# Twenty warm-up products instead of twenty-five, and a new order of work in the sixteen double steps of a gated attention mix

## The chip, the core and the metric

The kernel runs on one core of a Trainium2 chip. Its time is the device time of one execution in microseconds (us). The core has five engines that work side by side: TensorE (PE in the profile, with its weight loads as PEld), VectorE (DVE), ScalarE (ACT), GpSimd (POOL) and SyncE (SP, which here only issues DMAs). Each runs its own list of instructions in order, and they wait for each other by semaphores.

## The reference

Both branches read the same x (2048 tokens, 640 columns, 32 heads of 20):

```python
g = sigmoid((x * gate_w).sum(-1, keepdims=True))
# A: linear attention with softmax features
q, k, v = x @ wqkv                     # per head
phi(t) = concat(softmax(t @ w_phi), softmax(-t @ w_phi))
a = (phi(q) @ (phi(k).T @ v)) / (phi(q) @ sum(phi(k)) + 1e-6)   @ wo_A
# B: four segments of 512 tokens, with a memory M, z carried on
p     = softmax(q @ k.T * scale + causal mask)    # in the segment
a_mem = (phi(q) @ M) / (phi(q) @ z + 1e-6)        # phi(t) = t + 1 if t > 0 else exp(t)
o     = sigmoid(beta) * a_mem + (1 - sigmoid(beta)) * (p @ v)
M, z  = M + phi(k).T @ v, z + sum(phi(k))
b     = o @ wo_B
out   = g * a + (1 - g) * b
```

## The kernel before

The order of instructions on every engine is written out by hand; nothing is left to a scheduler.

**Start.** The weights of A's keys arrive by DMA in five blocks of rows (`wnat_k`), three from ScalarE's queue (blocks 0, 2, 4, line 98) and two from SyncE's (1, 3). While they travel, TensorE runs 25 products of zeros by zeros, 128x128 each, into two PSUM tiles in turn (`warm`, lines 316 to 318). Then a list of short names sets the order: T0 transposes block 0 (`wtp`, line 181), M0 multiplies it with the feature weights (`fold_ps`, line 189), and so on, each with a copy out of PSUM on ScalarE (a) or VectorE (d):

```python
for step in "T0a T2d M0a T1d M2a T4d M1a T3d X0 M4a M3a k0 g k1 v0 v1 r0 r1".split():
```

X0 transposes tokens (`xtp`), k and v are A's projections of keys and values (`pk`, `pv`, line 242). From k0 on TensorE runs through sixteen chunks of tokens, then A's sums (`kv_ps`), query features (`pq`) and numerators (`num`). All this is stage A, up to about 126 us.

**Stage B**, 127 to 303 us, is a loop over 16 double steps of two groups of four heads each (four double steps a segment). A double step has five bursts (`emit_burst`). A burst fills two PSUM tiles of two heads each with scores, `st_a` and then `st_b` (TensorE, line 757), and ScalarE takes exp of each (line 761, `PT`). As there are just these two tiles, the scores of the next burst wait, tile by tile, for the exps of this one. GpSimd cuts the triangles of the mask (line 768). After each burst TensorE gets filler work, and how much is written out by hand: `PLAN` has one string for each double step, a letter for each item, and `SHARES` has four numbers, the share of the double step's filler that is done after the first, second, third and fourth burst; the fifth takes the rest.

```python
whole = sum(w for w, _ in items)
for n, burst in enumerate(bursts(a, b)):
    burst()
    while items and (n == 4 or done + items[0][0] / 2 < SHARES[dstep][n] * whole):
        w, fn = items.pop(0)
        fn()
        done += w
```

The letters: `h` is half a projection of the next segment (five products of 128x320, line 943, and a copy out of PSUM on VectorE, line 949); `o` and `f` are halves of the output projections (line 887; copies and sums on VectorE, lines 896 and 898); they share two PSUM banks (`bps`). `A` and `B` are the weighted sums of v of the double step's first group and of the previous double step's last one (blocks 0 to 2, line 811), `D` and `C` their last block, the memory products (lines 819, 824) and the closing of the group (`emit_epi`: `rec`, `td` or `oB`, `mtmp` on VectorE, lines 836 to 854, all from the one PSUM tile `nda`). `k` and `q` put the exp of the key or query features on ScalarE (`ek`, line 915), `x` and `y` are the two VectorE operations that follow it (lines 918 and 919), `z` and `t` issue DMA transposes on SyncE's queue, and `u` four more at the end.

**PSUM.** In stage A a pool of four tiles of two banks is handed round (`aps`); the pools of later stages are laid over its banks in the order in which their names are listed (`num_pools`, line 594, and `b_pools`, line 712).

**After the last double step** the last group and the last four chunks of output are finished (303 to 314.8 us).

Of the kernel before, what the change touches and what calls it, by code (L numbers as in the profile page):

```python
# [15 lines left out]
def kernel(  # L16
# [84 lines left out]
    for what in "w1 w3 x0 g v0 v1".split():  # L101
        n = int(what[1:]) if len(what) > 1 else 0
# [72 lines left out]
    def w2tile(name):  # L175
        return aps.tile([P, 2, 512], F32, name=name, tag="w2")
# [137 lines left out]
        return omgh_b, CM  # L314

    warm = [w2tile("warm") for _ in range(2)]
    for n in range(25):
        nc.tensor.matmul(warm[n % 2][:, 0, 0:P], lhsT=zero_b, rhs=zero_b, start=True, stop=True)
    for step in "T0a T2d M0a T1d M2a T4d M1a T3d X0 M4a M3a k0 g k1 v0 v1 r0 r1".split():
        n = int(step[1:2] or 0)  # L320
# [259 lines left out]
    for what in "ppppvzppppdvp":  # L580
# [13 lines left out]
    nps_stack = ExitStack()  # L594
    num_pools = {n: nps_stack.enter_context(tc.tile_pool(
        name=n, bufs=2 if n == "pps" else 1, space=bass.MemoryType.PSUM, reuse_waits="tile"))
        for n in ('nps2', 'pps', 'nps0', 'nps1')}
    nps, pps = [num_pools[f"nps{n}"] for n in range(3)], num_pools["pps"]
    oTA = resB.tile([P, NCH + 1, KC, P], BF16, name="oTA")
    EARLY = 8  # L600
# [106 lines left out]
    with ExitStack() as bctx:  # L707
# [4 lines left out]
        bpt = bctx.enter_context(tc.tile_pool(name="bpt", bufs=2))  # L712
        b_pools = {n: bctx.enter_context(tc.tile_pool(
            name=n, bufs=2 if n == "bps" else 1, space=bass.MemoryType.PSUM, reuse_waits="tile"))
            for n in ('st_a', 'st_b', 'bps', 'bnd')}
        bps, st_a, bnd, st_b = [b_pools[n] for n in ("bps", "st_a", "bnd", "st_b")]
        st_pools = [st_a, st_b]

# [237 lines left out]
        def half_items(s, order):  # L956
# [11 lines left out]

        PLAN = ("qhhhhyzokxooAD", "qhhBhyChkzoxAooD", "qhhBhyChkzoxAooD",
                "ooBqoyoCokzxoADo", "hkhBhhChhqyhADztt", "khhBhxhqChfhyzAD",
                "khhBhxhqChfyzADt", "khhBhxhqChfyhzAD", "khhxtBhhqChyhADzt",
                "hhBhhqChfyhzAD", "hhBhhqCfhyzAthD", "hhBhhqhCftyhzAtD",
                "fBfCfftAD", "fBftCfftAD", "fBtfCffADf", "fBfCufAffD")
        SHARES = [[0.2, 0.42, 0.55, 0.77], [0.19, 0.4, 0.6, 0.85], [0.19, 0.4, 0.6, 0.8], [0.19, 0.4, 0.61, 0.79], [0.19, 0.38, 0.58, 0.8], [0.19, 0.41, 0.63, 0.86], [0.2, 0.4, 0.6, 0.83], [0.2, 0.4, 0.6, 0.83], [0.2, 0.4, 0.6, 0.8], [0.23, 0.39, 0.6, 0.82], [0.2, 0.39, 0.6, 0.82], [0.21, 0.39, 0.6, 0.82], [0.2, 0.4, 0.59, 0.8], [0.21, 0.39, 0.6, 0.8], [0.19, 0.37, 0.59, 0.81], [0.2, 0.41, 0.6, 0.85]]

        oT4 = oTA[:, 0:4]

# [7 lines left out]
        for dstep in range(NSEG * G // 2):  # L987
# [4 lines left out]
            items = []  # L992
            for w in PLAN[dstep]:
                if w in "hfo":
# [16 lines left out]
# [4 lines that stand above are left out]
# [156 lines left out]
```

## Time and profile before

| | us |
|---|---|
| three runs | 316.87, 316.88, 317.69; median 316.88 |
| the profiled execution | 316.55 |
| its span, first to last instruction | 314.8 |
| TensorE busy in the span | 303.3 (96%) |
| ScalarE busy | 252.2 (80%) |
| VectorE busy | 223.5 (71%) |
| GpSimd busy | 207.8 (66%) |

The granted TensorE clock of the profiled execution is 0.999. Around the span lie 316.55 - 314.8 = 1.75 us. TensorE's instructions are fetched in 33 packets of 16 KB (queue q8 of the profile). A row of the timeline gives start, length, engine, line, operation, names and count; "idle before" is how long the engine had been idle, and the name behind the arrow is what ended it.

### The profile page before, as it was taken

Reading aid. Unit: us, or ns where it says so; the run is one execution under the profiler, and the core shown is the slowest. Engines: PE = TensorE matmul, PEld = TensorE weight load, DVE = VectorE, ACT = ScalarE, POOL = GpSimd, SP = SyncE. Lnnn points to the kernel's source line nnn. Section 1 sums busy time; section 2 is a strip of 40 time slices with the busy share of each in tenths; the row PEclk is TensorE's granted clock in tenths of the full one; section 3 lists DMA queues with packets and bytes.
Section 4 is the critical chain, followed back from the end, with each engine's and each line's share of the span. In section 5 each row is a group of like instructions: output and inputs, shape, how many; then the busy total and the mean of one; then the engine's idle time right before and its main releaser. Section 6 shows DMA issues by size and latency. Waiting matters only on the chain.

```text
span 314.8 us, 10102 instructions
## 1 busy us (share of the span) xinstructions
PE 303.3 (96%) x4183; PEld 208.0 (66%) x4187; DVE 223.5 (71%) x508; ACT 252.2 (80%) x320; POOL 207.8 (66%) x308
## 2 busy tenths in 40 slices
PE   8999999999999999999999999999999999999994
PEld 7788877755578788465566566665666666566573
DVE  3487997998779997568767677876765765354562
ACT  4677888267856548999998999999899898998852
POOL 7588599004248989857647476888786867666550
PEclk9999999999999999999999999999999999999999
DMA  7979934439118889774421394474744544231132
GB/s 227 196 176 201 217 100 135 123 106 364 53 35 120 132 127 154 139 96 81 59 46 35 69 127 85 79 100 83 96 91 70 89 91 77 65 83 48 53 81 85
DMA packets 94008, 34.58 MB, mean 110 GB/s; under 512 B 82442, under 2 KB 93834, under 8 KB 93962
## 3 DMA queue, kind: packets, MB, share of 16 engines
q1 hardware_dynamic: 93386, 33.28, 53.6%
q8 instruction: 33, 0.54, 0.7%
q10 hardware_dynamic: 576, 0.66, 0.7%
q14 instruction: 13, 0.11, 0.1%
HBM read 6.10 MB, written 2.62 MB: 28 GB/s over the span
## 4 chain that ended last, share of the span: by engine, by line
PE 67%; ACT 22%; DVE 6%; POOL 2%; issue 2%; ACTq 0%; DVEq 0%; POOLq 0%
ACT PT L761 19%; PE st_ps L757 9%; PE proj L887 9%; PE proj L943 9%; PE pk L242 7%; PE pq L420 7%; PE pv L242 7%; PE nda L811 6%; PE proj L557 3%; DVE tt L527 2%; PE num L478 2%; DVE rr L503 2%; PE kv_ps L393 2%; POOL oA L686 1%; PE nda L819 1%
## 5 line engine op out<-in xcount | busy, mean ns | idle before, releaser
L761 ACT ACTIVATE PT<-st_ps 128x1024 bf16<-128x1024 f32 x160 | 153.7, 1023 | 12.6 <-PE st_ps L757 10.2
L768 POOL TENSOR_SCALAR_AFFINE_SELECT PT<-PT 128x512 bf16<-128x512 bf16 (+1 forms) x130 | 87.0, 688 | 45.6 <-ACT PT L761 45.4
L811 PEld LDWEIGHTS <-PT 128*128 128x128 bf16 x1280 | 40.0, 96 | 9.5 <-issue 5.6
L811 PE MATMUL nda<-vB,PT 128*128 128x21 bf16 x1240 | 41.6, 173 | 0.1
L261 POOL TENSOR_TENSOR EkSn<-Ek,krec 128x1280 bf16<-128x1280 bf16 x15 | 35.1, 2357 | 9.0 <-DVE krec L260 7.1
L949 DVE CAST Z<-proj 128x320 bf16<-128x320 f32 x44 | 21.0, 488 | 23.4 <-PE proj L943 22.5
L943 PEld LDWEIGHTS <-xTf 128*128 128x128 bf16 x300 | 26.4, 97 | 14.2 <-issue 5.7
L427 ACT ACTIVATE Eq<-pq 128x1024 bf16<-128x1024 f32 x20 | 19.4, 1021 | 12.3 <-PE pq L420 12.3
L257 DVE TENSOR_REDUCE ksum<-Ek 128x64 f32<-128x1280 bf16 x16 | 23.6, 1474 | 7.2 <-ACT Ek L253 7.2
L887 PE MATMUL proj<-WkA,oTA 128*128 128x320 bf16 x160 | 28.2, 300 | 0.0
L527 DVE TENSOR_TENSOR tt<-num,rr 128x640 f32<-128x640 f32 x32 | 24.9, 812 | 4.4 <-POOL rr L520 1.7
L686 POOL TENSOR_TENSOR oA<-tt 128x640 bf16<-128x640 f32 x16 | 24.6, 1541 | 5.2 <-DVE tt L527 5.0
L757 PE MATMUL st_ps<-Z 32*128 32x512 bf16 (+3 forms) x256 | 24.7, 299 | 3.2 <-ACT PT L761 2.2
L253 ACT ACTIVATE Ek<-pk 128x640 bf16<-128x640 f32 x32 | 20.8, 703 | 7.9 <-PE pk L242 6.8
L757 PE MATMUL st_ps<-Eq 32*128 32x512 bf16 (+3 forms) x256 | 25.1, 299 | 1.9 <-ACT PT L761 1.4
L242 PEld LDWEIGHTS <-xTf 128*128 128x128 bf16 x200 | 22.7, 113 | 4.7
L420 PE MATMUL pq<-xTf,WqA 128*128 128x512 bf16 x96 | 22.0, 379 | 0.4 <-issue 0.3
L851 POOL TENSOR_TENSOR oB<-td 128x320 bf16<-128x320 f32 x22 | 18.9, 861 | 5.0 <-DVE td L848 5.0
L887 PE MATMUL proj<-WvA,oT 128*128 128x320 bf16 x120 | 21.0, 300 | 0.0
L848 DVE TENSOR_TENSOR td<-nda,rec 128x640 f32<-128x640 f32 x23 | 19.0, 825 | 2.5 <-DVE rec L838 0.5
L557 PEld LDWEIGHTS <-xTf 128*128 128x128 bf16 x180 | 15.8, 97 | 4.6
L887 PEld LDWEIGHTS <-oTA 128*128 128x128 bf16 x160 | 13.6, 97 | 8.0 <-issue 4.0
(183 smaller groups left out, 553.5 us busy)
## 6 DMA issues: line engine op xcount, KB each, us to landing
Z<-EkSn SPq DMA_DIRECT2D x32, 160.0 KB, 2.7
out_dram<-orow SPq DMA_DIRECT2D x8, 160.0 KB, 1.8
out_dram<-oTA SPq DMA_DIRECT2D x6, 160.0 KB, 1.9
WvA<-in_A_wqkv_dram SPq DMA_DIRECT2D x2, 400.0 KB, 6.2
WvB<-in_B_wv_dram SPq DMA_DIRECT2D x1, 800.0 KB, 4.7
WkB<-in_B_wk_dram SPq DMA_DIRECT2D x1, 800.0 KB, 6.5
WqB<-in_B_wq_dram SPq DMA_DIRECT2D x1, 800.0 KB, 8.3
WkA<-in_A_wo_dram SPq DMA_DIRECT2D x1, 800.0 KB, 11.3
```

The source lines that it names most:

```text
L242: nc.tensor.matmul(ps[:, bk, 0:n], lhsT=key_tokens(c, sc), rhs=rhs, start=(c == 0), stop=(c == by_row[-1][0] if sc == 0 and W is WkA else ...
L261: (nc.vector if sc == NCH - 1 else nc.gpsimd).tensor_tensor(out=EkSn[:, sc].rearrange("p s (h f) -> p (s h) f", f=DH), in0=Ek.rearrange("p ...
L420: nc.tensor.matmul(pq[:, half, :], lhsT=WqA[:, c, j * P:(j + 1) * P], rhs=xq[:, 2 * qb + half, c], start=(c == 0), stop=(c == KC - 1))
L527: nc.vector.tensor_tensor(out=tt[:, sgn].rearrange("p (b h) d -> p b h d", b=2), in0=ps, in1=csb, op=ALU.mult)
L557: nc.tensor.matmul(ps, lhsT=xq[:, sc // 4, cc, sc % 4 * P:(sc % 4 + 1) * P], rhs=W[:, cc, half * 320:(half + 1) * 320], start=(cc == 0), s ...
L686: nc.gpsimd.tensor_tensor(out=oA.rearrange("p (h d) -> p h d", d=DH), in0=tt[:, 0], in1=tt[:, 1], op=ALU.add)
L757: nc.tensor.matmul(ps[:, i - i0, o:o + L - c * P], lhsT=kT[32 * i:32 * i + 32, c * P:(c + 1) * P], rhs=qT[32 * i:32 * i + 32, c * P:L], st ...
L761: nc.scalar.activation(out=PT[:, i0:i0 + 2], in_=ps, func=ACT.Exp, scale=SCALE_B)
L768: nc.gpsimd.affine_select(out=v, in_=v, pattern=[[0, n_i], [1, P]], compare_op=ALU.is_ge, fill=0.0, base=0, channel_multiplier=-1)
L811: nc.tensor.matmul(nd[:, j, i], lhsT=block(st, c)[:, i, (j - c) * P:(j - c + 1) * P], rhs=vB[:, c, 4 * st.g + i, :], start=(c == 0), stop= ...
L887: nc.tensor.matmul(ps, lhsT=oT[:, k % KC], rhs=W[:, k % KC, hs], start=(k == 0), stop=(k == n - 1))
L943: nc.tensor.matmul(ps, lhsT=xq[:, sc // 4, k, sc % 4 * P:(sc % 4 + 1) * P], rhs=W[:, k, half * 320:(half + 1) * 320], start=(k == 0), stop ...
```

## The change

- The loop of warm-up products runs 20 times, not 25. TensorE's list gets ten instructions shorter (a load and a product each), so that each border between packets of instructions falls ten instructions later in the work.
- The last warm-up product now goes to the other of the two `warm` tiles. Through the rest of stage A, banks 0 and 1 change places with banks 6 and 7 in every tile. In the lists of pools two names are exchanged (`nps1` with `nps2`, `bnd` with `st_a`), which gives the later pools the same exchange: every PSUM tile of after follows the same tile as before.
- `PLAN` is written anew in double steps 0 to 7, 11 to 13 and 15, and `SHARES` in all but 6 and 8. The letters are the same in sum. One `h` moves from double step 6 to 4, one `t` from 11 to 12. Seven times a letter with work for VectorE moves ahead of an item that ends with a copy out of PSUM: `y` ahead of an `h` in 0, 1 and 2, `x` ahead of an `o` in 2 and of an `h` in 5, 6 and 7. ScalarE's order of instructions stays as it is.

```diff
-    for n in range(25):
+    for n in range(20):
...
-        for n in ('nps2', 'pps', 'nps0', 'nps1')}
+        for n in ('nps1', 'pps', 'nps0', 'nps2')}
...
-            for n in ('st_a', 'st_b', 'bps', 'bnd')}
+            for n in ('bnd', 'st_b', 'bps', 'st_a')}
...
-        PLAN = ("qhhhhyzokxooAD", "qhhBhyChkzoxAooD", "qhhBhyChkzoxAooD",
-                "ooBqoyoCokzxoADo", "hkhBhhChhqyhADztt", "khhBhxhqChfhyzAD",
-                "khhBhxhqChfyzADt", "khhBhxhqChfyhzAD", "khhxtBhhqChyhADzt",
-                "hhBhhqChfyhzAD", "hhBhhqCfhyzAthD", "hhBhhqhCftyhzAtD",
-                "fBfCfftAD", "fBftCfftAD", "fBtfCffADf", "fBfCufAffD")
-        SHARES = [[0.2, 0.42, 0.55, 0.77], [0.19, 0.4, 0.6, 0.85], [0.19, 0.4, 0.6, 0.8], [0.19, 0.4, 0.61, 0.79], [0.19, 0.38, 0.58, 0.8], [0.19, 0.41, 0.63, 0.86], [0.2, 0.4, 0.6, 0.83], [0.2, 0.4, 0.6, 0.83], [0.2, 0.4, 0.6, 0.8], [0.23, 0.39, 0.6, 0.82], [0.2, 0.39, 0.6, 0.82], [0.21, 0.39, 0.6, 0.82], [0.2, 0.4, 0.59, 0.8], [0.21, 0.39, 0.6, 0.8], [0.19, 0.37, 0.59, 0.81], [0.2, 0.41, 0.6, 0.85]]
+        PLAN = ("qhhhyzhokxooAD", "qhhByhChkzoxAooD", "qhhByhChkzxoAooD",
+                "ooBqoyokCozxoADo", "hkhBhhChhqhyAhDztt", "khhBxhhqChfhyzAD",
+                "khhBxhhqCfyzADt", "khhBxhhqChfyhzAD", "khhxtBhhqChyhADzt",
+                "hhBhhqChfyhzAD", "hhBhhqCfhyzAthD", "hhBhhqhCftyhzAD",
+                "fBftCfftAD", "ffBtCfftAD", "fBtfCffADf", "fBCuffAffD")
+        SHARES = [[0.2, 0.42, 0.55, 0.78], [0.19, 0.4, 0.6, 0.84], [0.2, 0.4, 0.6, 0.81], [0.19, 0.38, 0.59, 0.78], [0.19, 0.38, 0.58, 0.81], [0.18, 0.41, 0.65, 0.86], [0.2, 0.4, 0.6, 0.83], [0.19, 0.4, 0.6, 0.83], [0.2, 0.4, 0.6, 0.8], [0.22, 0.39, 0.6, 0.82], [0.19, 0.39, 0.61, 0.82], [0.2, 0.39, 0.6, 0.82], [0.2, 0.4, 0.6, 0.8], [0.21, 0.4, 0.61, 0.8], [0.19, 0.37, 0.59, 0.82], [0.2, 0.41, 0.6, 0.84]]
```

## The prediction

> **What bounds the kernel.** The chain that ended last (section 4 of the page) comes first:
>
> ```profile
> PE 67%; ACT 22%; DVE 6%; POOL 2%; issue 2%; ACTq 0%; DVEq 0%; POOLq 0%
> ```
>
> It lies on TensorE for two thirds of the span, so I looked at the two places that the change touches. The first is the start, in the timeline of TensorE, 0 to 7.6 us:
>
> ```profile
> 1.06 2.85 PE L318 MATMUL warm<-zero_b 128*128 128x128 bf16 x25 [1.06 <-DVE zero_b L125]
> 3.70 1.27 PE L181 MATMUL wtp<-ident_b,wnat_k 128*128 128x128 bf16 x10
> 5.22 0.82 PE L189 MATMUL fold_ps<-Wphi,WkT 128*128 128x140 bf16 x10 [0.25 <-ACT WkT L183]
> 5.84 0.74 PE L181 MATMUL wtp<-ident_b,wnat_k 128*128 128x128 bf16 x5
> 6.37 0.76 PE L189 MATMUL fold_ps<-Wphi,WkT 128*128 128x140 bf16 x10
> 6.97 0.44 PE L181 MATMUL wtp<-ident_b,wnat_k 128*128 128x128 bf16 x5
> ```
>
> The transposes T0 and T2 follow the warm-up products without a hole, M0 waits for T0's copy, and five transposes take 0.74 us at 5.84 and 0.44 us at 6.97: between them TensorE got faster.
>
> The second place is stage B. The busy times of each engine in the stretches between the first exps of the double steps (columns: PE, PEld, DVE, ACT, POOL, clock, DMA share, GB/s; here double steps 3, 4, 6, 8, 10 and 12):
>
> ```profile
> 159.03:169.81 10.78, 10.42 (x155) 6.42 (x154) 8.33 (x22) 10.20 (x12) 6.44 (x12) 1.00 0.15 31
> 169.81:180.78 10.97, 10.74 (x159) 6.71 (x159) 6.24 (x16) 10.16 (x12) 6.67 (x14) 1.00 0.27 49
> ...
> 192.15:203.29 11.14, 10.67 (x165) 6.92 (x164) 8.31 (x18) 10.82 (x14) 8.91 (x14) 1.00 0.45 87
> ...
> 214.73:225.71 10.98, 10.23 (x161) 6.50 (x161) 8.12 (x18) 10.52 (x14) 9.10 (x15) 1.00 0.64 89
> ...
> 237.00:248.47 11.47, 11.37 (x170) 7.38 (x168) 7.71 (x17) 10.31 (x12) 8.42 (x15) 1.00 0.43 72
> ...
> 259.92:271.31 11.39, 11.37 (x167) 7.20 (x166) 5.35 (x12) 9.70 (x11) 8.47 (x17) 1.00 0.35 73
> ```
>
> TensorE and ScalarE are both nearly full. In 10 and 12 TensorE never rests and ScalarE does for 1.2 to 1.7 us; in 6 and 8, where ScalarE has two feature exps, it rests for 0.3 to 0.5 us. Neither engine alone sets the length. The timeline of ScalarE in double step 10 shows how:
>
> ```profile
> 237.00 1.94 ACT L761 ACTIVATE PT<-st_ps 128x1024 bf16<-128x1024 f32 x2 [0.20 <-PE st_ps L757]
> 239.53 3.87 ACT L761 ACTIVATE PT<-st_ps 128x1024 bf16<-128x1024 f32 x4 [0.59 <-PE st_ps L757]
> 243.29 0.74 ACT L915 ACTIVATE ek<-Z 128x640 bf16<-128x640 bf16 x1
> 244.09 1.94 ACT L761 ACTIVATE PT<-st_ps 128x1024 bf16<-128x1024 f32 x2
> 246.28 1.94 ACT L761 ACTIVATE PT<-st_ps 128x1024 bf16<-128x1024 f32 x2 [0.26 <-POOL Mbd L858]
> ```
>
> Two exps take 1.94 us, then ScalarE waits for scores when the filler before them was too long (0.59 us after the first burst). On TensorE the opposite: in the burst at 236.51 the four scores of the second tile wait 0.23 us for the exps before. Two rules follow. Where ScalarE was idle, filler that is d longer makes the next exps d later. Where a second tile waits for exps, filler restarts from their end, so lateness up to that wait is swallowed.
>
> **The start.** Five products go, 0.107 us apart (25 from 1.06 to 3.70): 0.53 us. Not all is on the path. The landing record of the first weight block is at 3.38, so T0 moves from 3.70 to about 3.41. The second block lands at 4.15, so T2 can begin at 4.20 rather than 4.23. M0 waits for the copy of T0, which goes from 4.48 to 4.19, so M0 starts at 4.93 rather than 5.22: 0.29 us. From the starts of single products a column costs 0.84 ns up to 6.87 us and 0.43 ns after. If that turn stays where it is, TensorE arrives there 0.27 us ahead in slow work, which is 0.14 us of fast work. I take 0.2 us, bounds 0.14 and 0.29. TensorE then works with no pause to 52 us (busy 42.86 of 42.86 us from 9.24 on), and the later inputs landed well ahead (tokens 6.79 for use at 7.91, values' weights 10.53 for 12.39 and later), so nothing swallows it.
>
> The Trainium skill (TensorE: Matmul & The Clock Gate, Why this matters for your kernels) asks for at least 4 us of unbroken work before the clock is released. By that rule of the Trainium skill the change would be wrong; the trace's turn came after products that ran without a hole from 1.06 to 4.77, 3.7 us, and 0.45 us of hole behind them, so it does not refute it. This is the second rival.
>
> **The exchange of banks and pools**: nothing. Every tile follows the same tile as before, so its waits are the same; what hides it is nothing, there is no work in it.
>
> **The packets' borders.** 33 packets of 16 KB are fetched, each in about 1 us. I looked at every start-to-start time on TensorE in stage B that exceeds its columns' time by 60 ns: each follows an exp, a VectorE copy, or is the fixed 0.1 to 0.2 us around a change to or from scores. No hole recurs at the spacing of 256 instructions. One hole in the whole trace (0.24 us at 61.3, beside a lost record) has no releaser. So the move costs 0, bounds -0.24 and +0.24.
>
> **Stage B, shares and letters.** The filler after each burst, counted by products (0.136 us for 320 columns, 0.025 us for 21, 0.037 us for 84), agrees with the trace within 0.02 us where nothing waits. The differences and what the two rules make of them, as lateness at the end of each double step:
>
> - 1: `y` (0.32 + 0.82 us of VectorE) moves from just ahead of C's closing to ahead of the third copy, where VectorE idled for 1.27 us; the closing starts 0.4 us earlier, and the wait of A's products for `mtmp` (0.09 us at 143.9) goes: -0.10. In 2 the same gain is swallowed.
> - 2: 0.05 us moves from the second filler to the first; ScalarE was not fed early enough there: +0.05.
> - 3: 0.14 us moves from the second filler to the fourth and fifth; a feature exp covers the first, so only the loss counts: +0.06.
> - 4: one `h` more, 0.68 us (+0.13, 0.15, 0.14, 0.18, 0.09 over the five bursts). Waits of second tiles (0.39, 0.32, 0.14 us) swallow part: +0.27.
> - 5: 0.14 us moves from fourth to third filler, but the next second tile waited 0.62 us: +0.01.
> - 6: one `h` less (-0.10, -0.17, -0.13, -0.14, -0.13). ScalarE idled before four of the five next exps: -0.36.
> - 7, 9, 10, 11: 0.10, 0.07, 0.10 and 0.05 us move from the first filler, which delayed exps, to the second, behind which second tiles waited 0.31 to 0.39 us: -0.32. The 0.14 us in 10 from fourth to third is swallowed by a wait of 0.18.
> - 0, 8, 12 to 15: within 0.04.
>
> Sum: -0.10 + 0.05 + 0.06 + 0.27 + 0.01 - 0.36 - 0.32 = -0.39. Bounds: if nothing of 4 and 6 cancels beyond what neighbouring rows show (8 has 6's new filler and two exps too and is 0.16 us shorter than 6; 12 has 4's new filler, without a feature exp, and is 0.42 longer than 4), the `h` costs 0.26 and the sum is -0.04. If also the waits for VectorE go (fillers lasted 2.6 us longer than their products in all, 0.57 of it in double steps 5, 7 and 10 alone), up to 1 us more is won.
>
> **The DMA queues.** `z` and `t` move past a turn or two of 2.7 to 3.3 us on SyncE's queue; the turned tiles are used a segment later. `u` moves ahead of an output: 0. The cost if that cover were gone is one such turn.
>
> **The sum.** -0.2 - 0.39 = -0.59, made against 316.55, gives 315.96 for the profiled execution; it was 0.33 under the median, so against 316.88: **316.3 us**, -0.19%. About 0.3% (0.95 us) is what a measurement of this kernel can tell from no change.
>
> **Rivals.** *A larger gain*: waits for VectorE go as well, as worked out above, 315.0 to 315.8. For it speaks that `x` and `y` now stand where VectorE was idle (22.5 us of waiting for h's products in the list of waits); against it, that few of those waits reach TensorE.
>
> *The clock turns later*, slower than before. Place: the first 10 us. TensorE now has holes of 0.22, 0.26 and 0.20 us before M0. If that keeps it slow beyond 6.87, everything streamed meanwhile costs double. Held to 9.24, where the unbroken stretch starts, that is 2.37 / 2 = 1.2 us; held to the end of k0 at 10.5, 1.8 us. It decides from a delay of 3.1 us on (1.55 us lost against 0.59 won). Time: 317.5 to 318.1. Against it: the holes between 3.46 and 6.87 add up to 0.45 us before and after. By the Trainium skill (the same page, Part 1: The HAM clock gate) the delay would be one window of 3.4 us, an estimated loss of 1.7 and 318.0 us; no run here shows such a delay.
>
> *VectorE holds up TensorE*, slower too. At the seven places where `x` or `y` moves ahead of a copy, the copy now waits for 1.14 us of sums, and if the feature exp is late, for that too. Two banks carry h, f and o, so TensorE is covered for one more item, 0.68 us; beyond it each place can cost 1.14 + 0.49 - 0.68 = 0.95 us. One at full price outdoes the gain (317.2), two give 318.2. For it: these items stand close together. Against: in double step 1 VectorE idles in front of exactly that copy.
>
> *It does nothing*: gains and losses in B cancel (the bound -0.04) and the start is worth 0.14 or less: 316.6 to 317.0.
>
> **Chances.** Forecast 0.40 (own range 315.8 to 316.7, of which 0.18 lies under 315.93), larger gain 0.22, nothing 0.11, clock 0.10, VectorE 0.17. Faster 0.18 + 0.22 = 0.40, same 0.22 + 0.11 = 0.33, slower 0.10 + 0.17 = 0.27. The range leaves out the ends of the larger gain and of the two slower cases: 315.0 to 318.2.
>
> **What would show it.** T0 at 3.4 and M0 at 4.9 us, the turn at 6.9, k0's first product near 9.0; double step 4 longer by 0.3 to 0.4, 6 shorter by about as much; first exps after the first burst of 7, 9, 10 and 11 earlier by 0.05 to 0.1. Transposes at 7 us that still take 0.74 us for five would prove the clock rival; new waits of `proj` for VectorE longer than 0.2 us the other. A different length of any stretch between 10 and 126 us would prove me wrong on borders or banks.

## Result, and the profile after

Median 315.32 us of 15 runs (314.72 to 317.12) against 316.70 of 15 runs of before (315.92 to 317.69). The medians differ by 1.38 us; the ratio of the means, with its 95% interval, is 0.9964 [0.9947, 0.998]: 0.36% faster, 1.1 us of 316.70. A second set of runs of the same kernel, beside other runs of before, gave 0.9951 [0.9936, 0.9966].

The page of after, queue q8 (TensorE's instruction packets; 33 before) and the chain that ended last:

```profile
q8 instruction: 32, 0.52, 0.7%
...
PE 70%; ACT 17%; DVE 5%; POOL 3%; DMA 2%; issue 1%; ACTq 0%; SPq 0%; DVEq 0%; POOLq 0%
```

One packet fewer is fetched within the span, and the chain has 2% of DMA in it. The longer of its two DMA pieces is a block of weights, seen in the timeline of TensorE, start of after, 0 to 6 us:

```profile
1.06 2.32 PE L318 MATMUL warm<-zero_b 128*128 128x128 bf16 x20 [1.06 <-DVE zero_b L125]
3.34 0.71 PE L181 MATMUL wtp<-ident_b,wnat_k 128*128 128x128 bf16 x5
5.30 0.71 PE L181 MATMUL wtp<-ident_b,wnat_k 128*128 128x128 bf16 x5 [1.25 <-DMA wnat_k<-in_A_wqkv_dram]
5.81 0.85 PE L189 MATMUL fold_ps<-Wphi,WkT 128*128 128x140 bf16 x10
```

T0 starts at 3.34 (3.41 was forecast), but T2 waits 1.25 us for the second weight block. This one execution (316.82 us, span 314.9) is not typical of the kernel; the profile of the repeated run shows the same rows without that wait:

```profile
3.41 1.46 PE L181 MATMUL wtp<-ident_b,wnat_k 128*128 128x128 bf16 x10
4.91 0.83 PE L189 MATMUL fold_ps<-Wphi,WkT 128*128 128x140 bf16 x10
5.53 0.74 PE L181 MATMUL wtp<-ident_b,wnat_k 128*128 128x128 bf16 x5
```

T0 at 3.41, M0 at 4.91, five transposes still in 0.74 us at 5.53: the rows that the prediction named. Stage B of after, busy times of each engine by double step (3, 4, 6, 8, 10, 12; columns as before):

```profile
160.42:171.17 10.75, 10.40 (x155) 6.42 (x155) 8.24 (x21) 10.16 (x11) 6.47 (x13) 1.00 0.14 27
171.17:182.37 11.20, 11.11 (x166) 7.34 (x164) 6.73 (x17) 10.20 (x11) 6.58 (x14) 1.00 0.26 48
193.68:204.45 10.77, 10.22 (x158) 6.48 (x158) 8.37 (x17) 10.55 (x13) 7.78 (x13) 1.00 0.52 75
215.80:226.76 10.96, 10.21 (x161) 6.49 (x161) 8.13 (x18) 10.51 (x13) 9.11 (x15) 1.00 0.57 89
237.99:249.49 11.50, 11.45 (x171) 7.44 (x169) 7.81 (x17) 10.32 (x11) 8.50 (x15) 1.00 0.41 72
260.76:272.14 11.38, 11.35 (x167) 7.18 (x166) 5.36 (x12) 9.69 (x10) 8.50 (x17) 1.00 0.27 62
```

Double step 4 is 0.23 us longer (10.97 to 11.20), 6 is 0.37 shorter (11.14 to 10.77); 10 did not get shorter. To see where the rest went, I cut every trace at the same six events (first `pk`, first `kv_ps`, first `num`, first exp of stage B, end of its last exp, end of the span), in us:

| | start to `pk` | to `kv_ps` | to `num` | to stage B | stage B | end | span |
|---|---|---|---|---|---|---|---|
| before | 9.24 | 46.11 | 33.09 | 38.35 | 176.61 | 11.43 | 314.83 |
| after | 10.65 | 46.11 | 33.02 | 38.46 | 176.00 | 10.70 | 314.94 |
| after, repeated | 9.03 | 46.09 | 33.57 | 38.51 | 175.99 | 10.70 | 313.89 |

Stage B won 0.61 us in both. The end won 0.73 us in both, and no line of the diff stands there. The start depends on the execution, and so does the stretch with A's sums (from `kv_ps` to `num`). The experiments below ask what won the end and what the start is worth.

### The profile page after: what moved, and what is told of

Its sections match the earlier page's. It is cut to its first block, busy times and chain, and to the rows that moved or that the text cites. A ratio compares the mean times of both kernels' runs of the same rounds, so it can differ in the third digit from the quotient of the medians.

```text
span 314.9 us, 10092 instructions
## 1 busy us (share of the span) xinstructions
PE 303.9 (96%) x4178; PEld 208.8 (66%) x4182; DVE 223.9 (71%) x508; ACT 252.0 (80%) x320; POOL 206.8 (66%) x308
## 4 chain that ended last, share of the span: by engine, by line
PE 70%; ACT 17%; DVE 5%; POOL 3%; DMA 2%; issue 1%; ACTq 0%; SPq 0%; DVEq 0%; POOLq 0%
ACT PT L761 14%; PE st_ps L757 10%; PE proj L943 10%; PE proj L887 9%; PE pk L242 7%; PE pq L420 7%; PE nda L811 7%; PE pv L242 7%; PE proj L557 4%; PE num L478 2%; DVE tt L527 2%; POOL oA L686 2%; DVE rr L503 2%; PE kv_ps L393 2%; DMA wnat_k<-in_A_wqkv_dram 1%
## 5 line engine op out<-in xcount | busy, mean ns | idle before, releaser
L768 POOL TENSOR_SCALAR_AFFINE_SELECT PT<-PT 128x512 bf16<-128x512 bf16 (+1 forms) x130 | 84.3, 668 | 46.7 <-ACT PT L761 46.3
L943 PEld LDWEIGHTS <-xTf 128*128 128x128 bf16 x300 | 26.4, 97 | 13.8 <-issue 5.3
L242 PEld LDWEIGHTS <-xTf 128*128 128x128 bf16 x200 | 22.7, 113 | 4.7
L836 DVE RECIPROCAL rec<-nda 128x32 f32<-128x32 f32 (+1 forms) x31 | 10.3, 331 | 12.8 <-PE nda L824 8.1
```

What stands on the lines that cost most here:

```text
L242: nc.tensor.matmul(ps[:, bk, 0:n], lhsT=key_tokens(c, sc), rhs=rhs, start=(c == 0), stop=(c == by_row[-1][0] if sc == 0 and W is WkA else ...
L768: nc.gpsimd.affine_select(out=v, in_=v, pattern=[[0, n_i], [1, P]], compare_op=ALU.is_ge, fill=0.0, base=0, channel_multiplier=-1)
L943: nc.tensor.matmul(ps, lhsT=xq[:, sc // 4, k, sc % 4 * P:(sc % 4 + 1) * P], rhs=W[:, k, half * 320:(half + 1) * 320], start=(k == 0), stop ...
```

## Experiments

Theory: the orders won 0.6 us in stage B, and the moved packet borders won 0.7 us at the end. Rivals: the orders did all of it; or five products' less time did it, or the exchange of banks.

### The two halves apart, and the whole again

Twenty products and all else as in after, with `PLAN` and `SHARES` of before (w20_old); and the reverse, 25 products and banks as in before with the new `PLAN` and `SHARES` (w25_new):

```diff
 # w20_old, against after
-        PLAN = ("qhhhyzhokxooAD", ...
+        PLAN = ("qhhhhyzokxooAD", ...          # and SHARES of before
 # w25_new, against after
-    for n in range(20):
+    for n in range(25):                        # and the pools' order of before
```

> Twenty warm-up products, but the orders and shares of before. If the two parts of the change add up as in the traces, the start gives 0.2 to 0.3 us where the second weight block lands early, stage B is as long as in before (176.6 us from its first exp to its last score step, double step 4 at 10.97, 6 at 11.14), and the ratio to before is 0.999. If the borders of the packets matter, the old orders lose time at the new borders: double steps differ from before by more than 0.1 us though their orders are the same.

> Twenty-five warm-up products and the new orders and shares. By the sum, stage B alone gains 0.6 us, ratio 0.998, and each double step is as long as in the trace of after (4: 11.20, 6: 10.77, 11: 11.27). By the rival of the borders the new orders were fitted to the new borders and lose here: 0.3 us or more over several double steps, ratio 1.000 or above. If most of the gain lies at the start, the ratio is 0.999.

> The changed kernel once more, for a second profile: the one on hand has the second weight block landing at 5.25 us. If that is a chance of the execution, T2 starts at 4.2 to 4.3 here, the clock turns near 6.9, stage B starts 0.2 to 0.5 us earlier than in before (126.3 to 126.6) and the span is 313.4 us. If twenty products lead to the late landing or to a late turn each time, T2 again starts after 5 us and the turn is after 8 us.

Measured, on one chip: w20_old 0.9962 [0.9949, 0.9975], w25_new 0.9990 [0.9977, 1.0003], after again 0.9951 [0.9936, 0.9966]. So the new orders alone can hardly be told from no change, and the border side carries most of the gain. Of the expectations, w20_old missed (0.999), and w25_new's 0.998 lies within its interval. after_again began as expected, but its stage B began at 127.2 us rather than 126.3 to 126.6, as its stretch with A's sums took 33.57 us. The cut traces:

| | start to `pk` | to `kv_ps` | to `num` | to stage B | stage B | end | span |
|---|---|---|---|---|---|---|---|
| w20_old | 9.07 | 46.12 | 32.86 | 38.37 | 176.64 | 10.69 | 313.74 |
| w25_new | 9.44 | 46.12 | 33.59 | 38.38 | 176.00 | 11.29 | 314.82 |

Stage B follows the orders to within 0.03 us, whatever the warm-up and the borders. The end follows the number of warm-up products, whatever the orders. The timeline of SyncE's queue, from 309 us on, before:

```profile
309.74 2.31 SPq L1120 DMA_DIRECT2D out_dram<-oTA  x3
312.15 0.41 SPq L1140 DMA_DIRECT2D out_dram<-oTA  x1
```

and w20_old:

```profile
309.38 1.31 SPq L1120 DMA_DIRECT2D out_dram<-oTA  x3
310.88 0.33 SPq L1140 DMA_DIRECT2D out_dram<-oTA  x1
```

Three output DMAs are issued in 2.31 us before and in 1.31 us after the move. In narrower stretches of the timeline of before, one of the three is the culprit:

```profile
309.74 0.33 SPq L1120 DMA_DIRECT2D out_dram<-oTA  x1
...
310.16 1.40 SPq L1120 DMA_DIRECT2D out_dram<-oTA  x1
311.66 0.40 SPq L1120 DMA_DIRECT2D out_dram<-oTA  x1
```

Issues take 0.33 to 0.41 us; the one at 310.16 takes 1.40. What else happens then? The DMA view of before, 309 to 312.6 us, by queue:

```profile
q1 hardware_dynamic: 286, 0.33, 26.4%
q10 hardware_dynamic: 144, 0.16, 13.1%
q8 instruction: 1, 0.02, 1.7%
```

The same view of w20_old has no q8 line. It is TensorE's 33rd packet, fetched from 310.18 us on for 0.99 us (the start and length of its record). The last output depends on the queue, not on VectorE, as the chains' last rows (VectorE, its last piece of output) show. Before:

```profile
310.89 0.32 DVE oTA L1139
```

w20_old:

```profile
310.53 0.33 DVE oTA L1139
```

Before, the data are ready at 310.89 + 0.32 = 311.21 and the issue comes at 312.15, 0.94 us later. In w20_old they are ready at 310.86 and the issue comes at 310.88.

### Borders without the time, and borders at the end alone

short_new has the time of twenty products and the borders of 25. tail_border is after, with five small products put in ahead of stage B's first filler projection: its borders lie as in after up to there, and as in before from there on.

```diff
 # short_new, against after (and the pools' order of before)
-    for n in range(20):
-        nc.tensor.matmul(warm[n % 2][:, 0, 0:P], lhsT=zero_b, rhs=zero_b, ...)
+    for n in range(25):
+        w = P if n < 18 else 32
+        nc.tensor.matmul(warm[n % 2][0:w, 0, 0:w], lhsT=zero_b[:, 0:w], rhs=zero_b[:, 0:w], ...)
 # tail_border, against after, in the first projection of double step 0
+                    while dummies:            # five of them
+                        dummies.pop()
+                        nc.tensor.matmul(ps[0][0:32, 0:32], lhsT=ident_b[:, 0:32], rhs=ident_b[:, 0:32], ...)
```

> The new orders with 25 warm-up products again, of which the last seven have 32 rows and columns rather than 128 and take about as long as two: the borders of the packets fall as with 25, the time at the start is as with 20. If only the time of the products counts, this is as fast as the changed kernel (ratio to before 0.996). If the borders count, it is as slow as 25 full products with the new orders.

> The changed kernel with five small extra products (32x32, overwritten by the real ones) ahead of the first projection of double step 0, where TensorE waits for ScalarE in any case. Up to there the borders of the packets fall as with 20 warm-up products, from there on as with 25. Theory of the borders: the fetch of a last packet at about 310 us is back in the span (33 fetches), the output DMA that SyncE issues beside it takes 1.2 to 1.4 us rather than 0.38, the stretch from the last exp to the end is 11.3 to 11.4 us rather than 10.7, and the gain against before shrinks by 0.6 to 0.7 us (ratio 0.997 to 0.998). Rival, that the end of the kernel is long by chance or by the length of TensorE's list alone: 10.7 us, and the time of the changed kernel.

short_new: 0.9985 [0.9968, 1.0001], against 0.9951 [0.9936, 0.9966] for after, on the same chip beside the same runs of before; the intervals do not meet. Its start (9.06) is that of twenty products, its end 11.39 that of 25. So it isn't the five products' time. tail_border: 0.9991 [0.9973, 1.001] (0.997 to 0.998 was expected), end 11.46, stage B 176.14 (double step 0 is 0.15 longer by the small products). The timeline of SyncE's queue in tail_border:

```profile
309.28 2.36 SPq L1125 DMA_DIRECT2D out_dram<-oTA  x3
311.73 0.41 SPq L1145 DMA_DIRECT2D out_dram<-oTA  x1
```

and its q8 row for 309 to 312.6 us:

```profile
q8 instruction: 1, 0.02, 2.2%
```

Ten instructions more (a load and a product each), some 185 us ahead of the end, bring the fetch and the slow issue back. That settles the end: in all four kernels in which the packet is fetched beside the outputs (before, w25_new, short_new, tail_border) the second of the four output issues takes 1.21 to 1.45 us, ends 0.37 to 0.40 us after the fetch does, and the end takes 11.29 to 11.46; in the ten others the four issues take 0.33, 0.38, 0.40 or 0.41 and 0.33 us, and the end takes 10.63 to 10.71. The exchange of banks has no part in it: tail_border has the banks of after and the long end, and w25_new has the banks of before and the stage B of after.

Not every issue beside a fetch grows. In the fourteen traces 28 output issues on SyncE overlap a fetch for TensorE by more than 0.05 us. The five that begin 0.09 us after the issue before them take 0.84 to 1.45 us and end 0.37 to 0.40 us after the fetch, as if they waited for it; the 23 that begin at least 1.85 us after the issue before them take 0.33 or 0.34 us. Whether outputs issued further apart would avoid the loss was not run.

### The warm-up's work, at borders beyond the end

If only the borders count, then longer products at the same count should do no harm, and fewer products should do no harm either. long20_new has twenty products of which five are 256 columns wide (the time of 25); wide10_new has ten of 256 columns (the time of 20, 20 instructions fewer); warm10_new has ten of 128 (the same list as wide10_new, half the work); wide12_new has twelve of 256. All have the new orders. long20_old is long20_new with the old orders, so that against before only the borders (and the banks) move.

```diff
 # long20_new, against after (wide10_new, wide12_new: r = 2 throughout, range(10), range(12))
+    zero_w = zero_b[:, None, :].to_broadcast([P, 2, P])
     for n in range(20):
+        r = 2 if n < 5 else 1
+        nc.tensor.matmul(warm[n % 2][:, 0, 0:r * P].rearrange(...), lhsT=zero_b, rhs=zero_w[:, 0:r], ...)
 # warm10_new, against after
-    for n in range(20):
+    for n in range(10):
```

> The changed kernel with twenty warm-up products, the first five of 256 columns: borders as with 20, time of slow work as with 25. If the shorter time of the warm-up is worth the 0.2 us of the forecast, this is 0.2 us slower than the changed kernel (ratio 0.996 to 0.997), first transposes at 3.7, k0 near 9.2 us. If time at the start is where the gain of the 20 lies, it loses about 1 us (ratio 0.999).

> The changed kernel with ten warm-up products of 256 columns rather than twenty of 128: the same time of slow work (2.13 us), but the borders fall another 20 instructions later, so that the border that lies in the query features (61 us) comes ten products of 0.22 us later. Theory of the borders: the hole there (0.0 to 0.6 us in the profiles with 20, 0.4 to 1.1 with 25) is gone, and the median is 0.2 to 0.4 us below that of the changed kernel (ratio 0.994). Rival, that the hole comes with the lost records or with the small products before it: it stays, and the time is that of the changed kernel.

> The changed kernel with ten warm-up products of 128 columns: half the time of slow work (1.07 us), borders as with the ten wide products. It tests the rival of the clock. If the turn depends on unbroken work before it, it comes after 8 us here and k0 starts 1 us later than with the wide ones (10 us rather than 8.9), ratio to before 0.997. If the turn comes at its own time whatever TensorE did (4.2 to 9.3 us in the profiles so far), k0 starts near 9 us and the time is that of the wide ones, ratio 0.994. The time of the products itself costs nothing either way, since the first weights land at 3.3 to 3.4 us.

> The new orders and shares as they are, with twelve products of 256 columns: the time of slow work between that of 20 and 25 (2.56 us), and the latest borders. It asks whether few wide products beat the changed kernel: if the borders in the sums of A (holes of 0 to 0.7 us there in every profile) still cost something with 20, the ratio is 0.994; if not, it is that of the changed kernel, 0.995 to 0.996.

> The kernel before with its own orders and shares and its own time of warm-up work (2.67 us), but in twenty products, five of them of 256 columns: nothing but the borders of the packets moves. Theory of the borders: 32 fetches in the span, no issue of an output DMA over 0.45 us, 10.7 us from the last exp to the end rather than 11.4, and a gain of 0.7 to 1.0 us (ratio 0.997), double steps as in before. If the gain of the twenty needs the shorter time, it is 1.000.

| | ratio to before | start to `pk` | first full-speed product | to `num` | stage B | end |
|---|---|---|---|---|---|---|
| long20_new | 0.9949 [0.9931, 0.9967] | 8.58 | 4.49 | 32.85 | 176.00 | 10.69 |
| wide10_new | 0.9940 [0.9924, 0.9955] | 8.93 | 6.77 | 33.52 | 175.99 | 10.69 |
| wide12_new | 0.9956 [0.9944, 0.9968] | 9.34 | 3.79 | 32.86 | 175.99 | 10.69 |
| warm10_new | 0.9986 [0.9973, 1.0] | 8.84 | 6.52 | 33.11 | 175.99 | 10.70 |
| long20_old | 0.9988 [0.9975, 1.0] | 8.98 | 6.06 | 33.45 | 176.62 | 10.71 |

(First full-speed product: the first transpose or feature product whose distance to the next falls from 0.84 to 0.43 ns a column.) Three things follow.

First, all five ends agree with after's 10.70.

Second, with the new orders the five products' time doesn't show: long20_new has the time of 25 and is as fast as after (0.9949 against 0.9951; 0.996 to 0.997 was expected). Where TensorE turns fast varies from one execution to the next, 3.79 to 9.32 us over all fourteen profiles, and so does the landing of the weight blocks (TensorE waits 0.90 us for one in wide12_new, 1.25 in after). The start to `pk` varies with both, 8.30 to 10.65. A gain of 0.2 us disappears in that.

Third, halving the warm-up's work cost 0.46% (warm10_new against wide10_new, intervals apart, though on different chips; best below, on warm10_new's chip and with more warm-up work, had 0.9961). By direction that is the second rival, a later turn to full speed. But the one profile of warm10_new turned at 6.52 us and was 1.06 us faster than the kernel's own median (314.83 against 315.89), so no trace shows the delay: measured in the times, not shown in its mechanism. wide10_new's 0.9940 is what was expected of it, but not for the reason given: its stretch with A's sums did not get shorter (33.52).

long20_old missed. The borders alone were to bring 0.997; they brought 0.9988, with the end at 10.71 as expected. Its interval reaches down to the 0.9977 that the end's 0.72 us is worth, but w20_old, which differs by the warm-up's time alone, had 0.9962. In the two profiles the whole difference of the spans (314.23 against 313.74) and more lies in the stretch with A's sums (33.45 against 32.86), and none at the start (8.98 against 9.07). That stretch differs as much between the two profiles of after (33.02 and 33.57). So what the five products' time is worth with the old orders stays open.

That stretch is the one place where borders show on TensorE itself. The timeline of TensorE around 61 us, before:

```profile
60.92 0.39 PE L420 MATMUL pq<-xTf,WqA 128*128 128x512 bf16 x1
61.59 1.69 PE L420 MATMUL pq<-xTf,WqA 128*128 128x512 bf16 x7 [0.28 <-issue]
```

short_new:

```profile
60.75 0.61 PE L421 MATMUL pq<-xTf,WqA 128*128 128x512 bf16 x2
62.07 1.25 PE L421 MATMUL pq<-xTf,WqA 128*128 128x512 bf16 x5 [0.72 <-issue]
```

Nothing that the profile shows ends these holes. They come at one position in TensorE's list whatever the work there (after 1466 loads and products, in some profiles 256 earlier), and end 1.29 to 1.61 us after the end of a packet's fetch. A's sums go through 256 small instructions, a packet's worth, in about 3.3 us. The hole at 1466 stands in the traces of the three kernels with 25 products' borders and in after_again. It is absent in the ten others, after among them, so one kernel has it in one execution and not in another; five of the ten (tail_border, long20_old, wide10_new, plan_only and the last kernel below) have one of 0.15 to 0.45 us at the earlier position. From the first sum to the end of the first query features the traces take 7.73 to 8.63 us; the rest of the stretch takes 25.1 in every one, so all of its scatter lies in the part with these two borders. Over all profiles the stretch takes 32.85 to 33.75; with 25 products' borders 33.09 to 33.75, with later ones 32.85 to 33.57. That they overlap is why its share of the gain stays open: some 0.26 us by the means of the two groups (33.48 of three, 33.22 of eleven), with a scatter of 0.7 within each.

### The new letters without the new shares, and a recombination

plan_only has the new `PLAN` with the old `SHARES`; one profile, since its double steps repeat to 0.02 us. The last kernel (best) has twelve wide warm-up products and the new orders, but the old `SHARES` in double steps 12 to 14 and the old third share (0.6) in 10, as the new ones had won nothing (13 and 14 together -0.04 + 0.05, 12 and 10 no shorter).

```diff
 # plan_only, against after: SHARES of before
 # best, against after: warm-up of wide12_new, and in SHARES
-  [0.19, 0.39, 0.61, 0.82], ... [0.2, 0.4, 0.6, 0.8], [0.21, 0.4, 0.61, 0.8], [0.19, 0.37, 0.59, 0.82]
+  [0.19, 0.39, 0.6, 0.82], ... [0.2, 0.4, 0.59, 0.8], [0.21, 0.39, 0.6, 0.8], [0.19, 0.37, 0.59, 0.81]
```

> The new PLAN with the shares of before, to tell letters from shares, by the lengths of the double steps (those of one order repeat within 0.02 us from profile to profile). By the working of the prediction the letters make 1 shorter by 0.05 to 0.1 (10.83), 4 longer (11.2), 6 shorter (10.77) and leave 7, 9, 10 and 11 as in before (11.45, 11.30, 11.46, 11.46), whose changes come from the shares. Rival for 11, which gained 0.19 rather than 0.05: the t that moved to 12 makes it shorter; then it is 11.3 here.

> Twelve warm-up products of 256 columns (2.56 us of slow work, few instructions), the new PLAN, and the new shares but for double steps 12, 13 and 14 (as in before) and the third share of 10 (0.60, as in before). From the profile with the old shares, 13 and 14 together are 0.10 us shorter (21.06 rather than 21.16). If moving 0.14 us from the fourth to the third filler of 10 was what cost there (11.50 rather than the 11.36 of the forecast), 10 is 11.36 to 11.40 and stage B 0.2 us shorter than in the changed kernel (175.8); if the first share is to blame, 10 stays near 11.46. Ratio to before 0.993 to 0.994, at or a little below that of the changed kernel.

Lengths of double steps (first exp to first exp):

| double step | 1 | 2 | 3 | 4 | 5 | 6 | 7 | 9 | 10 | 11 | 13 | 14 |
|---|---|---|---|---|---|---|---|---|---|---|---|---|
| before | 10.89 | 11.10 | 10.78 | 10.97 | 11.37 | 11.14 | 11.45 | 11.30 | 11.46 | 11.46 | 10.40 | 10.75 |
| plan_only | 10.83 | 11.08 | 10.69 | 11.39 | 11.25 | 10.79 | 11.45 | 11.30 | 11.47 | 11.46 | 10.46 | 10.60 |
| after | 10.84 | 11.10 | 10.76 | 11.20 | 11.31 | 10.77 | 11.35 | 11.23 | 11.50 | 11.27 | 10.36 | 10.80 |

Each half is worth about 0.3 us of stage B (176.61 before, 176.29 with the letters alone, 176.00 after). The letters won 1, 3, 5, 6 and 14 and lost in 13 and 4, in 4 more than expected (11.39 rather than 11.2). The shares won 7, 9, 11 and 13, took 4 from 11.39 to 11.20, and gave back what the letters had won in 3, 5 and 14, in part or whole. The `t` that moved out of 11 did nothing (11.46 with the letters alone). In best, 10 got shorter by 0.14 (11.36) and 11 longer by 0.16 (11.43): what was put right in one came back in the next.

The profile of best needs care. Its stage B is 177.27 us long, as double step 7 takes 12.70 instead of the 11.35 of the same order in after. There TensorE ran slow once more: the granted clock is 0.50 from 204.2 to 205.5 us, and its mean over the execution 0.995. Two of best's twelve runs have that mean, 315.87 and 316.01 us against the median of 314.96. The ratio of best, 0.9961 [0.9947, 0.9975], is no better than after's (0.993 to 0.994 was expected). None of the variants beats after beyond its interval; wide10_new (0.9940) is nearest.

## Why the prediction was right or wrong

**The number.** 316.3 was 1 us too high by the medians of the later runs (315.32), 0.6 by the ratio (0.9964 of 316.88 is 315.74). The measured median lies in the band given to the larger gain, but not for the reason given there, so that was luck: the rest came from a place that I had put at nothing. By the traces the terms of the sum gave some 0.8 us (0.2 and 0.6) rather than 0.59, and the end 0.73 us more.

**The step that failed** is the packets' borders, costed at 0 with bounds of 0.24 either way. The end alone gained 0.73 us, three times the bound. The reading was correct as far as it went: no hole recurs in stage B, and the traces confirm it: the double steps of one order repeat to 0.02 us at either position of the borders, but for double step 0 with tail_border's small products and best's 7. What failed was to look only for TensorE waiting for its own instructions. A fetch is also a transfer beside other DMAs, and the row that gave it away was in the trace of before: an output issue of 1.40 us among issues of 0.33 to 0.41, begun 0.02 us ahead of a q8 packet's fetch. The prediction's list of what would prove it wrong stopped at stretches up to 126 us and so left out the one that changed most. The other end of the same step, the hole at 61.3 us "beside a lost record", was a border's hole as well, and the stretch that it lies in, which the prediction had named as a sign, took 33.57 us in one of after's two profiles.

The Trainium skill (Runtime: NRT & Kernel Launch, Instruction fetch mechanics) calls the cost of crossing a block of 256 instructions mostly hidden. The traces agree for most of the 32 borders; at the last one the issue of 1.40 us instead of 0.38 disagrees, and at 61 to 63 us holes of 0.23 to 0.72 us.

**Stage B** was forecast at -0.39 and gave -0.59 by the first exps, of the right sign in all large terms:

| double step | 1 | 2 | 3 | 4 | 5 | 6 | 7, 9, 10, 11 | others | sum |
|---|---|---|---|---|---|---|---|---|---|
| forecast | -0.10 | +0.05 | +0.06 | +0.27 | +0.01 | -0.36 | -0.32 | 0 | -0.39 |
| measured | -0.05 | 0.00 | -0.02 | +0.23 | -0.06 | -0.37 | -0.32 | 0 | -0.59 |

The two rules (filler delays exps only where ScalarE idles; a second tile's wait swallows lateness) gave 6 and the group of four to 0.01. For the group that was in part luck: 7 and 9 gave what was forecast, but 10 gave +0.04 and 11 -0.19, where -0.10 and -0.05 were forecast. In 10 the gain of the first filler appeared: ScalarE's wait after the first burst fell from 0.59 to 0.49, and the second exps came 0.10 us earlier, 2.43 us after the double step's start. The third exps came later (4.53 rather than 4.46), since ScalarE now waits after the second filler, but that isn't the loss: best has the same 4.53 and takes 11.36. What failed is the 0.14 us from the fourth filler to the third, which the prediction had swallowed. The timeline of ScalarE in double step 10, after:

```profile
237.99 1.94 ACT L761 ACTIVATE PT<-st_ps 128x1024 bf16<-128x1024 f32 x2 [0.20 <-PE st_ps L757]
240.42 1.94 ACT L761 ACTIVATE PT<-st_ps 128x1024 bf16<-128x1024 f32 x2 [0.49 <-POOL oB L851]
242.52 1.94 ACT L761 ACTIVATE PT<-st_ps 128x1024 bf16<-128x1024 f32 x2 [0.16 <-PE st_ps L757]
244.34 0.74 ACT L915 ACTIVATE ek<-Z 128x640 bf16<-128x640 bf16 x1
245.12 3.08 ACT L761 ACTIVATE PT<-st_ps 128x1024 bf16<-128x1024 f32 x3
```

The 0.14 us more in the third filler make the fourth burst's exps later: they start 7.13 us after the double step's start (245.12), 7.09 before, but 6.99 in best, which has the old third share. The second tile of the fifth burst's scores waits for these exps, and the last filler follows. Those scores in the timeline of TensorE, before:

```profile
245.77 0.70 PE L757 MATMUL st_ps<-Z 32*128 32x128 bf16 x8
```

after:

```profile
246.66 0.84 PE L757 MATMUL st_ps<-Z 32*128 32x128 bf16 x8
```

and best (its double step starts at 237.31):

```profile
246.00 0.68 PE L759 MATMUL st_ps<-Z 32*128 32x128 bf16 x8
```

From the double step's start they end at 9.47, 9.51 and 9.37 us, which is its lengthening by 0.04 and its gain of 0.10. That they begin 0.10 us earlier in after than before, by the shorter fourth filler, wins nothing: they wait 0.14 us longer.

What double step 10 lost against its own term (0.14 us) came back in 11, so the group's sum held; best moved that amount from the one to the other again. The mis-sized terms are 2, 3 and 5, forecast 0.05 to 0.08 too long, and 1, 0.05 too short.

**The start** at -0.2 fits T0, M0 and `pk` (9.24 to 9.03 or 9.07), but the times can't tell it from nothing: long20_new loses nothing by the five products' time, and long20_old, which does, is no clean comparison. It is the least founded of the terms that seemed most certain.

**The rivals.** VectorE holding up TensorE: fell; every double step with `x` or `y` moved earlier kept its length or got shorter. Nothing: fell. The clock turning later: in after's own profile the turn did come late, at 9.32 us, behind the 1.25 us wait, and `pk` 1.6 us later than in the repeated profile (10.65 against 9.03), 0.9 of it M0's delay and the rest slow work behind it; but that was one execution in which a DMA landed late, and the repeated profile turned at 6.81. With half the warm-up its price (1.2 to 1.8 us) is about what warm10_new lost against wide10_new (0.46% of 316 us), though no trace shows the late turn there.

## What to carry to other kernels

When instructions are added or removed anywhere, the fetch of every later packet moves: look at what else each fetch then stands beside, the last outputs above all, and not only at the engine that fetches. A DMA issue that takes three times as long as its neighbours is such a mark, and a few small instructions more or fewer early in the list can test it. Where double steps repeat to 0.02 us, one profile settles an edit that no timing of whole runs can, if the granted clock stays up throughout.

## What was not expected of the hardware

- A packet fetch for TensorE beside an output DMA's issue on SyncE made that issue last 1.21 to 1.45 us instead of 0.38, in four kernels of four, and the last output was issued about 1 us later. It ended 0.37 to 0.40 us after the fetch, and of the output issues only those that followed another issue within 0.1 us grew.
- TensorE can stand still at a border when a packet's worth of small instructions runs in some 3.3 us: holes of 0.15 to 0.72 us, ending 1.29 to 1.61 us after the fetch's end. Why one execution of a kernel has the hole at 1466 and another has not (after_again and after) is open.
- The turn to full speed came between 3.79 and 9.32 us. before and w25_new run the same start up to M0 at 5.22 us in both, but the five transposes behind M0 take 0.74 us in before and 0.44 in w25_new.
- In best's profile the granted clock fell back to half in the midst of stage B, with TensorE busy for 11.44 of the 12 us from 192 to 204 us, and one double step took 1.35 us more. Why is open.
